# One fused fp32 kernel: two subtractions go from GpSimd to VectorE, and the hand-written order of all steps is written anew

## The chip, the cores and the metric

The kernel runs on one core of a Trainium2 chip. The metric is device microseconds for one execution; several executions are timed, and the median is compared. One more execution was recorded by the hardware profiler; all rows below come from it.

## The reference, cut to what matters

```python
def reference(x, state, moe_w_in, moe_w_out, moe_g_ln, moe2_w_in, moe2_w_out):
    y = attn(x, state)                  # 4 x 8 heads; two softmaxes, one over 32 states, one over 512 tokens
    y = y.transpose(0, 2, 1, 3).reshape(2176, 512)
    h = y @ moe_w_in                                   # 512 -> 1024
    solu = h * softmax(h)
    ln = layernorm(solu) * moe_g_ln
    z = ln @ moe_w_out                                 # 1024 -> 512
    h = z @ moe2_w_in                                  # 512 -> 2048
    g = h * tanh(softplus(h))
    return g @ moe2_w_out                              # 2048 -> 512
```

Everything is fp32.

## The kernel before, in words

An fp32 operand is split into a high part (a cast to fp32r) and a low part (operand minus high part), and a product is three matmuls: high by low, high by high, low by high. So nearly every operand that the PE takes costs a cast (mostly on ACT) and a subtraction (mostly on DVE) first. The host hands the weights over as 64-bit words, which `narrow` (L148 to L171) turns into fp32 in three or four steps on DVE and ACT; FLAGS B, T and W choose the engine and form of each.

The 2,176 tokens are 17 tiles of 128. For tile i, `a0(i)` is the matmul into `ph`, `a1(i)` the SoLU and LayerNorm (L557 maximum on DVE, L560 exponential on ACT, L562 product on DVE, L566 square on ACT, L568 to L572 small POOL steps, and the application to the 128x1024 tile: L580 on DVE where FLAGS N is 1, L575 on POOL and L577 on ACT where it is 0). `turn_far(i)` turns a tile through memory: L607 transposes 32x32 blocks on DVE into `tt`, L611 stores it (`td`), four L616 loads bring it back into `ln_l`, L618 casts to `ln_h` on ACT, L620 subtracts, 128x1024; FLAGS P chooses VectorE or GpSimd for that subtraction. `d(block, m)` multiplies with w_out (four quarters of six matmuls, L640) and copies the result out of PSUM (L645, `raw_a`, `raw_c`, `raw_d`; ACT or DVE by FLAGS X).

The second MoE layer runs in three passes over 6, 6 and 5 tiles, each with seven block products in place of eight. `x_split(pass, k)` makes the token operands (L811 difference, L816 cast on ACT, L818 subtraction on DVE). Pass 0 also prepares the 2 x 16 weight slices: `load64(0 or 1, f)` (L664, 512 KB from w2i or w2o, then narrow), `sums64` (L681), `split_in` and `split_out` (cast L705, L741 and subtraction L707, L743), `split_osum` (L748, L750, into `w2s`), and stores of the parts to device memory for passes 1 and 2, `keep_in` (L711) and `keep_out` (L754 for `w2s`, L757 for the rest). In a pass, for each of eight weight blocks: `hp` (L884, seven products of six matmuls into PSUM), `post` (L895 copies the first product to `m`, L898 and L901 add the next ones to `u`, L906 makes `c`), `act` (L918, L925 on ACT, L929), and `po` (L939 to L941 in pass 0, L989 to L996 later). The tile `m` of L895 may lie where `w2s` lay, so it must not be written before the stores of `w2s` have left it.

Nothing orders this work but two tables. FLAGS is a set of strings, a digit for each instance of an operation, read by `eng`, `on` and `copy_on`. ORDER is one string, two characters for an entry: each entry says which of the 1,040 step generators is advanced to its next `yield`. There are 3,182 entries. So each engine's queue, SP's DMA queue included, holds its instructions in the order of the table, and each engine takes its own queue strictly in order. A step is named here with its part: `turn_far(7).7` is the eighth part of that generator.

In the trace, 0 to 147 us are attention and the first layer (to tile 11), 147 to 222.7 us the last five tiles, the first x_split and the first weight slices, 222.7 to 340 us pass 0, 340 to 460 us pass 1 and 460 to 578 us pass 2.

Of the kernel before, what the change touches and what calls it, by code (L numbers as in the profile page):

```python
# [19 lines left out]
B, H, S, NS, D = 4, 8, 512, 32, 64  # L20
DM, FF1, FF2 = 512, 1024, 2048
NTOK = B * (S + NS)
P = 128
# [19 lines left out]
    A="1000",  # L43
    B="10101011000111100000000011100111",
    C="110000001000",
    D="00000",
# [20 lines left out]
    Y="00001111111111110",  # L67
    Z="11110111001100100",
# [10 lines left out]
    "CSBwCICWCZCSBwAsAsCJAuAuCSBwAwAwCWCSCJAyAyBuCZCZB0BuCWCWCWCLBuCLCJCaCdCWCLCWB0CaCJCLBwCGCGCTB0CWBwCdCdCaCICTBwCa"
    "BwCICaCaCTBxAlAlCeCXAnAnBxCaChApApCXArArBxCaCeB3CYCXB0ChChCaB3CeDMCYDMCHB3CeCICUCeCeCiDKDKCUCYCeCiB2CUCeB0B3CbCi"  # L80
    "CeDKDMCiB0CbB0CMB0CiCiDKCbDMB2B3CiCkB3CMCiB3CiB3CkCkB2DMCKClB5DKClDLCjCMB5DLClCjCgCKDLB5CgClClClCKCKDLCLCgAtAtCc"
    "B1ClAvAvDLCnAxAxCJCcClAzAzB1CcClCnCnB1B4B4CICqCoCMCICmCoCqCqCmCoCfDJCfDJCoCfCoCoCrDJDJCoB4CrCACjCoCjCoCrCjDPCjDP"
    "CmDJCpCACmCrDOCmCmCrCrDOCACpDOCrCrB9CjCrCtCjCsB9CtCtCsCmB9DPCuCwCmCuDPDOCuDPCMCwCwCMDOCuCuCuB6B6CxCuCuCzCuCxCNCz"
# [90 lines left out]
def attn_moe_kernel(ctx, tc, xT, xn, bd, stT, w_in, w_out, g_ln, w2i, w2o, out):  # L174
# [892 lines left out]
    def plan(step, *args):  # L1067
        steps.append((step, args))
# [71 lines left out]
    for ps in range(NPASS):  # L1140
# [93 lines left out]
```

## Time and profile before

| | us |
|---|---|
| runs | 575.02, 576.29, 577.04 |
| median | 576.29 |
| the profiled execution | 580.88 |
| its span, first to last instruction | 578.0 |
| PE, DVE, ACT, POOL busy in it | 557.9, 506.4, 355.6, 58.5 |

The profiled execution is 4.6 us above the median of the runs, and 2.9 us of it lie outside the span. Matmuls are pipelined and overlap in the records, so a busy PE isn't a PE at its peak; it is the stretches in which it isn't busy that can be read directly. A row of the time line is: start, duration, engine, line, operation, output and inputs, shape, count, and in brackets the idle time of the engine just before it with what ended it.

### The profile page before, as it was taken

The page shows a single profiled execution, that of the slowest core. Times are in us where ns is not written, and L with a number is a line of the kernel's source. Part 1 is how long each engine was busy: PE and PEld are TensorE (multiplying, and loading weights), DVE is VectorE, ACT ScalarE, POOL GpSimd, SP SyncE. Part 2 cuts the span into 40 slices and gives each one's busy share as a digit, 9 for nine tenths or more (in the row PEclk, how much of TensorE's full clock was granted, in tenths as well). Part 3 has the DMA queues.
Part 4 walks back from the last instruction along what each step waited for, and adds up shares of the span by engine and source line. Part 5 has one row for each costly group of instructions (what it writes and reads, how often), then busy time and mean ns, then how long its engine had stood idle before and what let it go on. Part 6 is the DMA issues. An engine that isn't in the chain of part 4 may idle for free.

```text
span 578.0 us, 9801 instructions
## 1 busy us (share of the span) xinstructions
PE 557.9 (97%) x3513; PEld 493.5 (85%) x3513; DVE 506.4 (88%) x956; ACT 355.6 (62%) x662; POOL 58.5 (10%) x132
## 2 busy tenths in 40 slices
PE   9899999999999796999999999999999999999997
PEld 4444877799689796888989989999999998999997
DVE  6999988984779686999999998679889999989996
ACT  6998966555467544999989774553334634533331
POOL 0003314121122000000000000000000015000023
PEclk9999999999999999999999999999999999999999
DMA  8962234053216777898999797967677679898842
GB/s 343 411 219 74 74 112 170 13 183 110 74 74 220 234 283 273 292 305 314 335 370 341 281 338 266 372 221 269 237 270 261 227 280 322 296 333 301 280 161 91
DMA packets 50015, 139.18 MB, mean 241 GB/s; under 512 B 5680, under 2 KB 22704, under 8 KB 49968
## 3 DMA queue, kind: packets, MB, share of 16 engines
q1 hardware_dynamic: 49968, 138.57, 67.7%
q8 instruction: 27, 0.44, 0.3%
q14 instruction: 20, 0.16, 0.1%
HBM read 98.18 MB, written 40.37 MB: 240 GB/s over the span
## 4 chain that ended last, share of the span: by engine, by line
PE 68%; DVE 13%; ACT 9%; DMA 6%; issue 2%; POOL 1%; SPq 0%; ACTq 0%; POOLq 0%; DVEq 0%
PE hp L884 27%; PE pm L640 8%; PE po L989 6%; PE po L990 6%; PE po L991 6%; PE po L940 3%; PE po L941 3%; PE po L939 3%; PE ph L548 3%; DMA w<-in_w2i 2%; ACT ph L566 2%; DVE ez L562 1%; DMA ko<-w2s 1%; PE po L1057 1%; DVE ez L580 1%
## 5 line engine op out<-in xcount | busy, mean ns | idle before, releaser
L884 PE MATMUL hp<-xo,w2r 128*128 128x384 f32 (+1 forms) x504 | 93.3, 329 | 0.3 <-DVE c L906 0.3
L884 PE MATMUL hp<-xo,w2swh 128*128 128x384 f32 (+1 forms) x336 | 83.8, 332 | 3.9 <-ACT m L895 3.9
L884 PEld LDWEIGHTS hp<-xo,w2r 128*128 128x128 f32 x504 | 84.3, 188 | 3.5 <-DVE c L906 1.1
L640 PE MATMUL pm<-ln_l,gw_hi 128*128 128x256 f32 (+1 forms) x256 | 76.3, 298 | 5.6 <-ACT raw_d L645 4.6
L640 PE MATMUL pm<-ln_h,gw_hi 128*128 128x256 f32 (+1 forms) x256 | 74.8, 292 | 0.0
L640 PE MATMUL pm<-ln_h,gw_lo 128*128 128x256 f32 (+1 forms) x256 | 74.5, 291 | 0.0
L996 DVE TENSOR_TENSOR acc<-po,acc 128x384 f32<-128x384 f32 (+1 forms) x136 | 68.7, 522 | 3.7 <-PE po L991 3.1
L884 PEld LDWEIGHTS hp<-xo,w2swh 128*128 128x128 f32 x336 | 60.7, 191 | 6.2 <-ACT m L895 4.2
L925 ACT ACTIVATE gh<-c 128x384 fp32r<-128x384 f32 (+1 forms) x57 | 29.2, 513 | 51.8 <-DVE c L906 44.1
L640 PEld LDWEIGHTS pm<-ln_l,gw_hi 128*128 128x128 f32 x256 | 48.2, 188 | 9.5 <-ACT raw_d L645 5.4
L884 PE MATMUL hp<-xo,w2swl 128*128 128x384 f32 (+1 forms) x168 | 55.8, 332 | 0.0
L963 ACT CAST qh<-t 128x384 fp32r<-128x384 f32 (+1 forms) x60 | 28.6, 489 | 37.5 <-PE po L991 21.4
L640 PEld LDWEIGHTS pm<-ln_h,gw_hi 128*128 128x128 f32 x256 | 48.2, 188 | 0.5
L906 DVE TENSOR_TENSOR c<-hp,u 128x384 f32<-128x384 f32 (+1 forms) x72 | 38.2, 532 | 11.9 <-PE hp L884 11.7
L640 PEld LDWEIGHTS pm<-ln_h,gw_lo 128*128 128x128 f32 x256 | 48.6, 190 | 0.0
L548 PE MATMUL ph<-swh,aT 128*128 128x512 f32 x128 | 45.1, 455 | 2.3 <-DVE swl L506 1.3
L989 PE MATMUL po<-ql,w2oh 128*128 128x384 f32 (+1 forms) x120 | 39.4, 328 | 0.2 <-DVE acc L996 0.2
L990 PE MATMUL po<-qh,w2oh 128*128 128x384 f32 (+1 forms) x120 | 38.8, 323 | 0.0
L991 PE MATMUL po<-qh,w2ol 128*128 128x384 f32 (+1 forms) x120 | 38.7, 323 | 0.0
L548 PEld LDWEIGHTS ph<-swh,aT 128*128 128x128 f32 x128 | 22.4, 188 | 14.2 <-issue 5.6
L965 DVE TENSOR_TENSOR ql<-t,qh 128x384 fp32r<-128x384 f32 (+1 forms) x59 | 31.1, 537 | 1.3 <-ACT qh L963 0.9
L884 PEld LDWEIGHTS hp<-xo,w2swl 128*128 128x128 f32 x168 | 32.0, 190 | 0.0
(458 smaller groups left out, 1349.1 us busy)
## 6 DMA issues: line engine op xcount, KB each, us to landing
w2r<-ki SPq DMA_DIRECT2D x16, 768.0 KB, 6.2
w2ol<-ko SPq DMA_DIRECT2D x15, 768.0 KB, 5.9
w2oh<-ko SPq DMA_DIRECT2D x15, 768.0 KB, 6.1
w<-in_w2i SPq DMA_DIRECT2D x16, 512.0 KB, 5.7
w2swh<-ki SPq DMA_DIRECT2D x8, 896.0 KB, 7.2
w2swl<-ki SPq DMA_DIRECT2D x8, 896.0 KB, 5.5
td<-tt SPq DMA_DIRECT2D x12, 512.0 KB, 2.7
ln_l<-td SPq DMA_DIRECT2D x48, 128.0 KB, 3.1
```

Source lines behind the costliest of these rows:

```text
L548: nc.tensor.matmul(out=ph[:, hf * 512:(hf + 1) * 512], lhsT=a_[:, c * P:(c + 1) * P], rhs=w_[:, q, hf * 512:(hf + 1) * 512], start=q == 0 ...
L640: nc.tensor.matmul(out=pm[:, :n], lhsT=w_[:, k, m * P:(m + 1) * P], rhs=l_[:, c0:c0 + 4 * len(blk), k, :], start=k == 0 and j == 0, stop=k ...
L884: nc.tensor.matmul(out=r, lhsT=w_[:, 0, k * P:(k + 1) * P], rhs=x_[:, k, :n], start=s in (0, 1, 3, 4) and cnt == 0, stop=cnt == 5, skip_gr ...
L906: nc.vector.tensor_tensor(out=c, in0=bank[ps, fp, s], in1=u, op=ALU.add)
L925: nc.scalar.activation(out=gh, in_=src, func=AF.Mish)
L939: nc.tensor.matmul(out=po["p", j], lhsT=gh[:, c], rhs=wl, start=first, stop=False)
L963: nc.scalar.copy(out=hi, in_=src)
L965: on('V', ((ps - 1) * NFP + fp) * 4 + int(name[1]) - 1).tensor_tensor(out=lo, in0=src, in1=f32(hi), op=ALU.subtract)
L989: nc.tensor.matmul(out=r, lhsT=wh[:, a, c], rhs=x[1], start=first or not held, stop=False)
L990: nc.tensor.matmul(out=r, lhsT=wh[:, a, c], rhs=x[0], start=False, stop=False)
L991: nc.tensor.matmul(out=r, lhsT=wl[:, a, c], rhs=x[0], start=False, stop=last or not held)
L996: on.tensor_tensor(out=o, in0=x, in1=y, op=ALU.add)
```

## The change

The same 1,040 steps are made, and ORDER has the same 3,182 entries in another order: no step is added or left out. One loop that lists the steps gets a condition on `STAGED`, which is empty, so the list stays the same. The digits of FLAGS that change move instances between engines: the two L620 subtractions that were on GpSimd (P, tiles 4 and 11) and one L965 subtraction (V) go to VectorE; of the L580/L577 applications tiles 3 and 11 go to VectorE and tiles 10, 14, 15 and 16 to ScalarE (N); five L564 (Z) go from GpSimd to VectorE; seven more L645 copies go from ScalarE to VectorE (X); the first two L895 copies go from ScalarE to VectorE (M); slice f=0 of w2i and the last w2o slice change the form of narrow (T).

```diff
 FLAGS = dict(
-    B="10101011000111100000000011100111",
+    B="00011111001011100001000001101110",
...
-    M="001000000010000001100000",
-    N="00000001101001111",
+    M="110000000001101000010000",
+    N="00010001100101000",
...
-    P="00001000000100000",
-    Q="101111011011110101010001",
+    P="00000000000000000",
+    Q="111011101111111101010001",
...
-    S="110011",
-    T="11001001100000001000111111111110",
+    S="101000",
+    T="11001001100000000000111111111111",
...
-    V="0000000000000000000000000001000000000000000000000000000000000000",
-    W="00100000000100100001101001000111",
-    X="01000000100000000001000000000100",
+    V="0000000000000000000000000000000000000000000000000000000000000000",
+    W="00000000011000000001100001001101",
+    X="00100000111100101001010000000101",
...
-    Z="11110111001100100",
+    Z="10000101000001001",
...
 ORDER = (
-    "AAAABIBIBKBKBQBQATBSBSBMBMARARAUAUBABABJBJBJBCBCBLBLBJBLBOBOBRBRAWAWATBLBWADADBRA-A-BTBTBXAJAJBTA0A0BNBRANANAYAY"
+    "AAAABKBKATBIBIBQBQBSBSBMBMBCBCBABAARARBLBLATAUAUBLAWAWBJBJBLBJBOBOBRBJBRANANBWBRA-A-BTBWADADBXBTA0A0BRAJAJBNBXBN"
...
         for fp in range(NFP):
-            if ps:
-                for d in range(2):
+            for d in range(2):
+                if ps or fp in STAGED:
                     plan(s_fetch_in, ps, fp, d)
+                if ps:
                     plan(s_fetch_out, ps, fp, d)
```

On DVE near 95 us, where the first of the two subtractions was made on POOL beside L580, the queue before was (L580 is the application to tile 7, L607 the block transpose, L506 the low part of the state weights, L557 the maximum of the next tile, L620 at the end that of another tile):

```order
L607 STREAM_TRANSPOSE tt<-ez 128x1024
L506 TENSOR_TENSOR swl<-ph,swh 128x2x512
L580 TENSOR_SCALAR ez<-ez,lnsm 128x1024
L607 STREAM_TRANSPOSE tt<-ez 128x1024
L506 TENSOR_TENSOR swl<-ph,swh 128x2x512
L557 TENSOR_REDUCE lnsm<-ph 128x1
L620 TENSOR_TENSOR ln_l<-ln_l,ln_h 128x1024
```

and now is

```order
L607 STREAM_TRANSPOSE tt<-ez 128x1024
L506 TENSOR_TENSOR swl<-ph,swh 128x2x512
L580 TENSOR_SCALAR ez<-ez,lnsm 128x1024
L607 STREAM_TRANSPOSE tt<-ez 128x1024
L620 TENSOR_TENSOR ln_l<-ln_l,ln_h 128x1024
L506 TENSOR_TENSOR swl<-ph,swh 128x2x512
L557 TENSOR_REDUCE lnsm<-ph 128x1
L620 TENSOR_TENSOR ln_l<-ln_l,ln_h 128x1024
```

One L620 more stands on DVE, between the transpose of tile 7 and the subtraction L506 for which the PE waits.

On DVE near 180 us, at the tiles 15 and 16 (the last L607 of each list is the transpose of tile 15, the L562 and L564 that of tile 16's statistics), the queue before was

```order
L557 TENSOR_REDUCE lnsm<-ph 128x1
L811 TENSOR_TENSOR raw_a<-raw_a 128x2x384
L580 TENSOR_SCALAR ez<-ez,lnsm 128x1024
L562 SCALAR_TENSOR_TENSOR ez,lnsm<-ph,ez 128x1024
L818 TENSOR_TENSOR xo_2016<-raw_a,xo_2016 128x768
L564 TENSOR_SCALAR lnsm<-lnsm 128x1
L607 STREAM_TRANSPOSE tt<-ez 128x1024
```

and now is

```order
L557 TENSOR_REDUCE lnsm<-ph 128x1
L811 TENSOR_TENSOR raw_a<-raw_a 128x2x384
L607 STREAM_TRANSPOSE tt<-ez 128x1024
L818 TENSOR_TENSOR xo_2004<-raw_a,xo_2004 128x768
L562 SCALAR_TENSOR_TENSOR ez,lnsm<-ph,ez 128x1024
L620 TENSOR_TENSOR ln_l<-ln_l,ln_h 128x1024
```

The application to tile 15 (L580) has left DVE for ACT, and the transpose of tile 15 stands ahead of the work on tile 16.

At the start of pass 0 the row of ACT before was (L816 the last x_split, L895 the first product to `m`, L705 casts of the next weights, L925 and L918 the first activation)

```order
L816 CAST xo_2520<-raw_a 128x768
L895 COPY m_2529<-hp 128x384
L705 CAST w2r<-w_2445 128x256
L925 ACT_TABLE_LOAD
L925 ACTIVATE gh<-hp 128x384
L918 ACTIVATE a__2554<-hp 128x384
```

and DVE's, in which L153 to L169 narrow the slice `load64(0, 3)`,

```order
L645 COPY raw_d<-pm 128x384
L153 TENSOR_SCALAR w_2445<-w_2445 128x512
L160 TENSOR_SCALAR w_2445<-w_2445 128x512
L165 SCALAR_TENSOR_TENSOR w_2445<-w_2445 128x512
L169 SCALAR_TENSOR_TENSOR w_2445<-w_2445 128x512
L818 TENSOR_TENSOR xo_2520<-raw_a,xo_2520 128x768
L898 TENSOR_TENSOR u_2542<-hp,m_2529 128x384
```

DVE's now is

```order
L645 COPY raw_d<-pm 128x384
L818 TENSOR_TENSOR xo_2499<-raw_a,xo_2499 128x768
L895 COPY m_2521<-hp 128x384
L707 TENSOR_TENSOR w2r<-w_2372,w2r 128x256
L707 TENSOR_TENSOR w2r_2502<-w_2372,w2r_2502 128x256
L153 TENSOR_SCALAR w_2452<-w_2452 128x512
L898 TENSOR_TENSOR u_2538<-hp,m_2521 128x384
```

The copy L895 has gone from ACT to DVE, right behind the last x_split, and the slice `load64(0, 3)` is narrowed behind it. By where the tiles lie, `m` there now overlaps another `w2s`, whose store left much earlier; the later one lies under the tile `u` that L901 writes.

## Rows read from the trace of the kernel before

**Rows 1.** By stretch: PE, weight loads, DVE, ACT, POOL busy; granted clock, DMA share, GB/s.

```profile
222.70:236.00 13.30, 9.41 (x45) 8.95 (x44) 8.98 (x20) 7.50 (x13) 0.00 (x0) 0.87 0.73 277
236.00:340.00 104.00, 103.59 (x514) 92.50 (x513) 102.08 (x221) 93.19 (x161) 0.00 (x0) 1.00 0.92 326
340.00:460.00 120.00, 120.00 (x673) 117.22 (x672) 103.78 (x203) 58.04 (x124) 1.02 (x1) 1.00 0.74 266
```

**Rows 2.** Time line near 95 us: POOL's subtraction, DVE beside it, PE.

```profile
95.19 2.41 POOL L620 TENSOR_TENSOR ln_l<-ln_l,ln_h 128x1024 fp32r<-128x1024 f32 x1
95.20 2.95 DVE L580 TENSOR_SCALAR ez<-ez,lnsm 128x1024 f32<-128x1024 f32 x1 [0.90 <-POOL lnsm L572]
100.59 0.72 PE L548 MATMUL ph<-swh,aT 128*128 128x512 f32 x2 [1.30 <-DVE swl L506]
106.64 0.81 DVE L580 TENSOR_SCALAR ez<-ez,lnsm 128x1024 f32<-128x1024 f32 x1 [0.20 <-POOL lnsm L572]
```

**Rows 3.** Time line 146 to 155 us: start of x_split, and POOL's second subtraction.

```profile
146.57 0.83 ACT L816 CAST xo<-raw_a 128x768 fp32r<-128x768 f32 x1 [1.93 <-PE tr L483]
147.43 0.96 DVE L818 TENSOR_TENSOR xo<-raw_a,xo 128x768 fp32r<-128x768 f32 x1 [6.36 <-ACT xo L816]
152.23 1.23 DVE L620 TENSOR_TENSOR ln_l<-ln_l,ln_h 128x1024 fp32r<-128x1024 f32 x1
153.37 4.02 DVE L818 TENSOR_TENSOR xo<-raw_a,xo 128x768 fp32r<-128x768 f32 x2
154.13 2.45 POOL L620 TENSOR_TENSOR ln_l<-ln_l,ln_h 128x1024 fp32r<-128x1024 f32 x1 [19.00 <-ACT ln_h L618]
```

**Rows 4.** Pieces of the chain that ended last, in order of time: start, us, what.

```profile
163.77 1.24 ACT ez L577
182.48 4.23 DMA td<-tt
186.73 6.72 DMA w<-in_w2i
220.97 7.20 DMA ko<-w2s
```

**Rows 5.** Time line 175 to 200 us: tiles 15 and 16, and who waits.

```profile
175.47 1.12 ACT L566 ACTIVATE ph<-ez,lnsm 128x1024 f32<-128x1024 f32 x1 [1.56 <-DVE lnsm L564]
181.22 1.23 DVE L607 STREAM_TRANSPOSE tt<-ez 128x1024 f32<-128x1024 f32 x1
193.53 0.67 ACT L155 ACTIVATE w<-w 128x512 f32<-128x512 f32 x1 [4.79 <-DMA w<-in_w2i]
196.82 0.39 PE L640 MATMUL pm<-ln_l,gw_hi 128*128 128x256 f32 x1 [2.69 <-ACT raw_d L645]
```

**Rows 6.** Time line 207 to 222 us: SP's issues, PE at block 7, DVE.

```profile
207.27 0.33 SPq L664 DMA_DIRECT2D w<-in_w2o  x1
207.70 0.38 SPq L711 DMA_DIRECT2D ki<-w2swh  x1
211.92 0.34 PE L640 MATMUL pm<-ln_l,gw_hi 128*128 128x384 f32 x1
211.97 0.43 DVE L153 TENSOR_SCALAR w<-w 128x512 f32<-128x512 f32 x1 [1.52 <-DMA w<-in_w2o]
221.14 0.55 DVE L645 COPY raw_d<-pm 128x384 f32<-128x384 f32 x1
```

**Rows 7.** Time line of the start of pass 0, and one stretch of it.

```profile
224.45 0.43 DVE L153 TENSOR_SCALAR w<-w 128x512 f32<-128x512 f32 x1 [2.76 <-DMA w<-in_w2i]
228.32 0.48 ACT L895 COPY m<-hp 128x384 f32<-128x384 f32 x1 [4.19 <-DMA ko<-w2s]
228.85 0.62 PE L884 MATMUL hp<-xo,w2swh 128*128 128x384 f32 x2 [3.89 <-ACT m L895]
230.00:232.00 2.00, 2.00 (x7) 2.00 (x7) 1.07 (x4) 1.83 (x4) 0.00 (x0) 0.50 0.97 348
233.65 0.51 PE L884 MATMUL hp<-xo,w2swh 128*128 128x384 f32 x2
```

More of the change, by code (lines that the diff above doesn't have):

```diff
@@ L79 @@
[L79 to L83, printed above, removed]
@@ new lines @@
+    "AgA3A5BjBjA5AiAiA9BdBhBhA5CDAdAdA5BnBnBFCDBdAfAfBiBiCCBrCEBFBdBkBHCCByBHBdCEBHBvBFBdCECCByBHBFBvCDByBlAhAhCEBeAj"
+    "AjBUBsBsBvBeBVCRBUBlAkAkCFBtAmAmBwBVBtCFAoAoCFCHCRCRAqAqBtCFCHBtCHCGCFCSBtCVCHCGBtCSBtCVCVBtBtCSCEBwCECWBzBzCSCS"
+    "CSCIBwCWCZCSBwAsAsCLAuAuCSBwAwAwCWCSCLAyAyBuCZCZCJBuCWB0CJCWCWBuCaCJCdCWCLCWB0CaCJBwCLCGCGB0CTBwCWCdCdCaCICTBwCa"
+    "BwCICaCaCTBxAlAlCeCXBxAnAnCaChApApCXBxCaArArCeCXChChB3CaCeCYB0CUCYB3DMCUCeCHB3DMCICeCeB0DKCiDKB3CeCeB2CYCiCUCMCe"
+    "DMCMCiB2DMCKDMCiCbB3CiCiDKB0B0DKB0CbCiCkB2DKCiCbCiCkCkB3B3B3DLClB5CjClDLCMCjClB5CgDLCKB5ClDLClClCKCKDLCnCgClAtAt"
@@ new lines @@
+    "B1AvAvCgB1ClAxAxCnCnClAzAzB1B4CqCoB4CLCcCmCoDJCICJCqCqCmCoCMCcCIDJCoCrCoCoCfDJB4CfCoCrDJCfCcCACoCmCoCrCmCmDPCmDJ"
+    "CpDPCjCrCACjDOCjCrCrCACjDOCpDOCrCrB9CmCrCtCsB9CmCtCtCsCjB9DPDOCuCwDOCjCuDPCuCwCwDPCuCuCuB6B6CxCMCzCuCuCxCNCMCzCz"
+    "B7CNCNCxCNDQCPDQB-DQCPC0CPDQCPB7DNC0CNCuDNDQC0DNDSB7DNB-B7DSCpDNB-CsDSC0B7CpC0C0DSCpCvCpDUB-CsC0CsB-DUCsC0B7C0Cv"
+    "DUB-B7B7C2CPCxB8CxCxB-B-DUB8DSCxC2C2CpB8CxCxDUDRCpDTCsCyDRDTC1CyDTCsC1CQDRCQC3DRDTDRC3CQCvDTCOCvC3DXCyCOCyDXCvC3"
+    "CvCOCOC3C3CyDXCyB_CQDXC3C3B_DYDXB_DYC3DVCvC4DYDVCyCvC4DVCyDYDVDYDWDVDWDWDWCQDpDpDqDqDqDbC1DtCQDWC1C5C1DvDtC1C4Dt"
@@ new lines @@
+    "DtDvC4DbC4DvDvC4C5DuDbDuDaC1DuDuC5C1C4C5C5C4DbC6C8DbC6C8C8C6DcC6C9DaC6C6DcC9C6DaC6C_C9C6C_C_C7C9C9C9DcC7DAC9C9Dc"
+    "C9DCDADcC-DCDCDAC-DaDADDDZDaDADADZDZDDDADZDADDDFDAC7C7C7DDDBDFDFC7DDDDC-C-DZC-DdDDDGDrC-DdDBDDDDDwDeDdDGDED0D1Dd"
+    "C7DrDrDeDEDxDeDdDGC-DeDwC7DfDGDGDGDfDeC-DfD0DGDfD0DgDfD1DgDGDGD0DgD0DgD1D8DhD1DBDgDxEBEBDwDwDhDBDjDED1DBDjD2D-DE"
+    "D2DBDjD2DED8D9DEDHD2D2ECECDhD9D_EFEFDjD-DyEDEDDxDhDjEGEGDxDiDhDxDBDkD_DiDEDBELEHEHDID3DkDED4DiDHDiDHDyDyDkDiD3Dy"
+    "DkDyDmDkDIDzD5DzDmDzDzDzD6DIDlD7D6ELEAEADlD4D7EMDlELELDlD5ELEIEEEEDmETDlEYEYETDmEcEcDnDmEMEMDnEMEIDnEMENEVDnENEZ"
@@ new lines @@
+    "EZENENENEUDoEWEUDnEaEaEVDoEJEIEdEdEWDoEIEfEeEeDoEIDoGpGpDsEOGrEPEXDsDsGrGsEjEPEiGrEOE5EJEJEbGsGtEJGrEJEfGtEKEfEQ"
+    "GrEKEfGsEKGrGtEREKEKGsGyGyESEREjGrGrEXEXGsEgGwESGvGxGxGwGsGsGzGzGvEQGuE2GvG9EbEbEjGuEiEjEfG9GwElEiG3G3GuEiG5G5Ej"
+    "G-G2G2EsEiE5G1G1EwEwEsEqG0G0ElE0E0EgG-G7G7EvEvEmEqFQE2G8G8EgEzEzEkG9EgEkEkEkEkG6G6ErE2EtEgG4G4G_ErExExG9G_FREhE2"
+    "E6EhG9EhG-EnG_EoG9G-FQEoHCG9G9G-HCEhEhHBHFHFEmEpE2E3HDHDHBEuEuE5G-G-HEHEE5FQHPEpFQHBHPE5HQFRFBHJHJHQFRFGFGEtHPE9"
+    "HCHAE1E1HAEnHPFQHRFNHREyEyHAHLHLFYHRHPFRHQFdFdFYHHHHE6FBFhFhE8HGHGFRFKFKE3FFE9HIHIFaE8E6HMHMFJE3E6FnHQHPFeFeFSFS"
@@ new lines @@
+    "E3HOHOE6HKHKE7FDE3FNHPHPFHFHFNHUE4FNE4HWHWE7E4HNHNHQE-E_HVHVHQHQFoHUE4E4HhE7HTE_HTHXHXFAE-FOE7E7FCFFFFHhFAHiFCFk"
+    "HSHhFJFJFnHTFDFEHcHcHiFnFLFLFEHdHdFIFIHSFnFNFMFMHhHSFTI7HbHbFUHiHjHZHZFoFTFSHYHYHjHUFZFOHhFSFSFOFZHhFOHiF-FnHhHh"
+    "FbHjFkHiFfFfHoHoFOHmHmHiHiHaHaHlFbHnHnHlFUFkFjFjHzFPHkFPFPFkI7HgHgI7HfHfFWHlFVHeHeFWHkFPFPH0HtHtFaFlFXHzFoFvF_Hm"
+    "FcFcFoHzF0F0H0FiFiFVFXHpHpH1FoH1F7HvHvFgFgF-F-HzFpFxFvF-F1F1HzH0F4F4H1FlHzH0HkH4HzHzI7H4I7H0HrHrFxH3HqHqH3FkF5F5"
+    "HsHsFpFrFpFqHuHuH0H0FwFzFrH6H6H2H3HyHyFqH2I7F3IFI7FlFpFpIAIAFlH2H5H5FwFyHwHwGVFlIGF2F2HxHxFyFsFmH-H-GWFmF6F6FmH7"
@@ new lines @@
+    "H7F-FtH_H_F_F_FsIBIBFmFmF_FtH9H9H4F8FuIFF7I7I7F7FzFzF_IFF7FuIGIEIEGSGGF3F3F7IDIDIHGLGLGAGIIFGAIHGMGMGIGCGVIFGQGQ"
+    "IGGVGAIHIFGBGVIGGAGAIFIFGBIKGGGHH8H8IGGPGPIKGHICICIJIGIGIJIMIMIKGJGWIXIIGNGNIJIIF8F8ILILGWIIF8ISISGVIRIRGCGWF8IN"
+    "INF9IPIPIYF9GdF9IVIVGWGiGiGEITITF9F9GSGXIQIQGSGEIWIWGFGXGTGdGfIXGXGSGmGmGJGjGjIXIYGRGRGDGXGXGeGKGKGFIOIOIZGSGgIX"
+    "GDIZGkGkGYGOGOIZIXGZGhGeIYIUIUGYIXIYGlGgIcIfIfIcGZGoGoIcIXIXIYGTIbIdIdGTJDJDIbIYIYJFJFIeIeGTIbIpGfIaGnGnGTIaIjIj"
+    "JiIaGaIlIlI8GUGUIqIiIiGUGUGUGbIkIkGcGbIgIgGhGhGcIpGaI8I8GlGlIpJAIqJAJAIpIrJAJAIrI8I8IoIoIqJBImImI9JBJBIpI9I9JBJB"
@@ L131 @@
+    "PIO5O4O7PJO6O7PIO6PNPNO8PJPIPIPNPMO8PMPDPDQAQAPJPJO9PMP-PLPlP-P-POPOPPPlPmPOPOPOPlPRO9PSPRO-PmO_O-PlPPPiPQPiPiPQ"
+    "PePePkO_PTPkPkPmPUPTPdPdPUPnPVPnPSPWPVPlPWPnPlPmPlPlPmPpPXPmPmPpPYPXPoQCPqPrPqPYPZQDPrPaPsPZQCPqPpPbPaQCPrQDPuPs"
+    "PgPgPbPcPuPfPfPtPcPwQBQBPtPxP_P_PwQCPxQEQEPrPrPyQEPvPzPvQCQDPyQCQDPyPzP0QDP1PzP0QGP6P1QGP2QHQGP7QHP2P3QHP4P4P3P8"
+    "P5P5P4QCQCP4QIP5QDQDP9QFP5QIQFQJP6QIP6P7QKQJQFQJP7QLP8QKQMP5QKP9QOQLQMP4QLQNQMQPQNQNQOQPQOQP"
 )
```

73 lines of the change are left out of this document (22 added, 51 removed).

## Prediction

> **What bounds the kernel now.** I read the stretches first, then the time line of each stretch in which the PE isn't busy, then the chain that ended last between them. The span is 578.0 us. From 236 us on the PE has no time to give: 103.59 us of 104 in pass 0, 120.0 of 120 in pass 1 [rows 1]. Pass 0 is tight on three sides: DVE is busy 102.08 of its 104 us and the DMA engines 0.92 of the time [rows 1]. So work saved inside the passes can't show, and a new wait there costs its full length. What can be won lies ahead of 236 us, in a few places where the PE stands still, and above all between 222.7 and 236 us, where it is busy 9.41 of 13.30 us and its granted clock means 0.87 [rows 1].
>
> Those places hang together. Between 147 and 229 us the chain runs from the last tiles' transposes through DMAs: the store of `td` takes 4.23 us, the weight slice that takes its room 6.72, and the store of `w2s` for which pass 0 waits 7.20 [rows 4]. ACT stood 4.19 us at L895 for that store (its tile `m` lies where `w2s` lay), and the PE 3.89 us behind it, for the second part of `hp` [rows 7]. After that gap the granted clock was 0.50 in the stretch 230 to 232 us, the lower level of 1.2 GHz [rows 7].
>
> **The change part by part.** The sum is a difference of waits, read in the profiled execution (span 578.0, 580.88 in all) and taken off the median of 576.29: the two differ by 4.6 us, which I take to be the same before and after.
>
> (a) *First subtraction back to DVE.* L620 took 2.41 us on POOL from 95.19, and the L580 that DVE began at 95.20 took 2.95 us, where the same shape took 0.81 at 106.64 [rows 2]. So DVE lost 2.14 us to a neighbour. On DVE the subtraction costs 1.23 [rows 3], and it stands ahead of the L506 for which the PE waited 1.30 [rows 2]: 2.14 − 1.23 = 0.9 us earlier, at most the 1.30 that the PE waited. Take 0.9.
>
> The Trainium skill, page "SBUF — State Buffer", section "Who interferes with whom", says that VectorE and GpSimd share one pair of ports, and that whoever begins first holds it for its whole instruction while the other is blocked. The trace agrees in the main: 2.14 us lost beside an instruction of 2.41. By the rule L580 would have lost all 2.41, and this term would be 1.2 in place of 0.9.
>
> (b) *Second subtraction.* At 154.13 it took 2.45 on POOL, while two L818 on DVE took 4.02 together; one alone took 0.96 [rows 3], so 2.1 was lost; on DVE it costs 1.23. Up to 0.9 earlier, but in the new order the tile's other steps stand between, so I count nothing, and keep 0.9 for the range.
>
> (c) *Start of x_split.* ACT waited 1.93 us for the PE's transposition L483 before the cast at 146.57, and DVE had idled 6.36 behind it [rows 3]. Now that transposition stands three quarters of a `d` block earlier in the PE's queue. That is longer than the wait ahead of the cast, so at most the 1.93 can go, and something else may be last then. Between 0 and 1.9, take half: 1.0.
>
> (d) *Tile 15 applied on ACT.* Its square ran at 175.47 for 1.12, to 176.6 [rows 5]. A cast of x_split (0.83) stands behind it on ACT, and the small POOL steps end about 1.2 us behind the square, as tile 12's did ahead of its L577 at 163.77; so the application, 1.24 [rows 4], runs from 177.8 to 179.0, and the transpose, now ahead of the next tile's work, follows at 179.0 in place of 181.22 [rows 5]: 2.2 us earlier. Store and slice load follow in chain [rows 4]. ACT waited 4.79 us at 193.53 for that slice, and the PE 2.69 at 196.82 for a copy that stood behind it on ACT [rows 5]; nothing stands in the way of passing the 2.2 on. Range 0 to 2.2.
>
> (e) *What is queued anew at 207 to 213 us.* In SP's queue the load of a w2o slice stood ahead of the store L711 (207.27, 207.70); now it stands behind it, and L711 waits for ACT's last `split_in`: some 0.8 us later. And `d(7, 1)`'s copy L645, on DVE before and now, has moved from the end of this stretch (221.14) to ahead of that slice's first step L153, which ran at 211.97 [rows 6]. The PE makes its last quarter now in the slot that began at 211.92 [rows 6] and ends about 213.0; then comes the copy. So DVE, whose queue holds the weights behind it, starts 1.6 us later, and up to 2.4 with the later load; the store of `w2s` follows. If the PE arrives early it costs nothing. Between 0 and −2.4, take −2.0, near the upper end, since the PE is held in the same chain as DVE.
>
> (f) *Start of pass 0.* L895 moves to DVE, right behind the last x_split, and its `m` lies over a `w2s` stored long before; now the L901 of the same block has to wait for the late store, and it is first needed by the sixth part of `hp`. Before, that part began at 233.65 [rows 7]: 5.5 us behind the landing (220.97 + 7.20 = 228.17). Now it can begin 0.1 + 0.6 (L901) + about 1.0 of DVE's queue behind the landing, at 1.7. That is 3.8 us, with the clock's fall in it, since parts three to five then run before the landing, with a gap of about 1 us in place of 3.89. L895 costs DVE 0.55 us twice where DVE idled 2.76 us shortly after (224.45) [rows 7].
>
> (g) *Everything else.* Seven L645 copies, two L895, five L564 and one L965 more on DVE, less the applications: counted operation by operation with the durations of their kind (0.55 for a copy [rows 6]), some 3 us of DVE work more and 2 of ACT's, spread over the span, and none more on DVE in pass 0. In pass 1 DVE has 16 us to spare in 120 [rows 1]. Counted at nothing, cover: that slack.
>
> Sum: 0.9 + 1.0 + 2.2 − 2.0 + 3.8 = 5.9 us; 576.3 − 5.9 = **570.4**.
>
> **The rivals.** *The start is won and pass 0 gives it back.* Pass 0 has its own clock: 326 GB/s at a DMA share of 0.92 [rows 1]. If what paces it is the remaining slice loads and the stores, DVE idles as the head start runs out. Against it: DVE itself has only 1.9 us idle there, so loads come in time. That gives back all but a remnant: 575 to 577.
>
> *Only the start of pass 0 counts*: (c) and (d) end in DMAs that share the engines and land no earlier, and (e) is not paid. 576.3 − 3.8 = 572.5, which lies in the forecast's range.
>
> *New waits in pass 0: slower.* ORDER is new throughout, and large reads are issued at other points. The price of a slice that comes late is the 2.76 us for which DVE stood at 224.45 [rows 7], and in pass 0 with DVE 98% busy each such wait goes to the end. Two of them (5.5) leave it just faster; from the third it is slower: 576.3 − 5.9 + 8.3 = 578.7. For it: the DMA at 0.92 has no room for a late start. Against it: DVE's work and its place among the loads is nearly the old one there.
>
> **How the numbers follow.** Forecast, with the case of (f) alone, 0.73; gain given back, 0.14; new waits, 0.13. What this kernel's runs can tell from no change is about 0.3%, 1.7 us: below 574.6 is faster, above 578.0 slower. Likely range: 0.9 to 1.3 from (a), 0 to 0.9 from (b), 0 to 1.9 from (c), 0 to 2.2 from (d), −2.4 to 0 from (e), 3.8 from (f): gains of 2.3 to 10.1, so 566.2 to 574.0. The range takes in the gain given back, to 577. Faster 0.73, same 0.14, slower 0.13.
>
> **What would show it.** In the profile after: (a) no L580 near 95 us above 0.9 us, and no PE wait of 1.3 at the next L548; (c) the L816 cast earlier than 146.57 by more than (a) brings; (d) the store of tile 15 near 178 us less (a) and (c), and ACT's 4.79 us wait shorter; (e) a DVE wait for the PE at L645 before 213 us; (f) no `hp` wait above 1.5 us and a granted clock of 1.00 in 222 to 236 us, with `hp`'s sixth part about 6 us earlier. Pass 0's length should stay at 104 us. The forecast is wrong if DVE shows DMA waits in pass 0 that sum to more than 3 us, or if the late store's landing moves later than 228.2.

## The result and the profile after

| | us |
|---|---|
| before, median | 576.66 (575.02 to 578.66) |
| changed, median | 570.32 (569.96 to 570.45) |
| ratio | 0.9887, 95% interval 0.9855 to 0.992 |
| profiled execution before, span | 580.88, 578.0 |
| profiled execution after, span | 570.37, 568.6 |

The change takes 6.3 us off the median; the prediction said 5.9 and 570.4. Between the two profiled executions the spans differ by 9.4 us. So the trace of before shows some 3 us more to win than its median, and that has to be explained too.

First, two stretches of the kernel before that [rows 1] doesn't have (length, then busy time of PE, weight loads, DVE, ACT and POOL, granted clock, DMA share, GB/s):

```profile
95.00:110.00 15.00, 13.06 (x88) 9.32 (x73) 13.50 (x16) 7.42 (x14) 3.69 (x6) 1.00 0.20 76
194.00:204.50 10.50, 6.78 (x55) 6.44 (x54) 9.14 (x15) 8.35 (x15) 0.00 (x0) 1.00 0.85 273
```

And the stretches of the changed kernel, to be held against these two and [rows 1]:

```profile
95.00:110.00 15.00, 15.00 (x107) 11.37 (x106) 13.03 (x17) 8.33 (x16) 2.33 (x8) 1.00 0.29 103
194.00:204.50 10.50, 10.50 (x72) 10.48 (x71) 10.29 (x20) 5.36 (x12) 0.00 (x0) 1.00 0.74 276
222.70:236.00 13.30, 12.43 (x62) 10.92 (x62) 12.69 (x29) 12.25 (x20) 0.00 (x0) 1.00 0.92 333
236.00:340.00 104.00, 103.25 (x515) 92.23 (x514) 101.51 (x219) 93.30 (x167) 0.00 (x0) 1.00 0.89 323
340.00:460.00 120.00, 120.00 (x683) 118.15 (x683) 103.62 (x204) 55.88 (x116) 0.00 (x0) 1.00 0.76 274
```

From 95 to 110 us and from 194 to 204.5 us the PE doesn't stand still any more (1.94 and 3.72 us before), and between 222.7 and 236 us its clock is granted in full (1.00 in place of 0.87). From 236 us on hardly anything has changed: DVE and PE are as full as before. The time from the start of the sixth part of `hp(0, 0)` to that of the last addition of the kernel is 341.0 us before (233.65 to 574.69) and 341.2 after (223.89 to 565.04). All of the gain lies ahead of that part, as the prediction had it.

The start of pass 0, against [rows 7]. The prediction calls the part of `hp` that waited 3.89 us there the second; twelve matmuls, two parts of six, stand ahead of it in the trace, so it is the third.

```profile
217.57 0.55 DVE L895 COPY m<-hp 128x384 f32<-128x384 f32 x1
218.17 0.62 PE L884 MATMUL hp<-xo,w2swh 128*128 128x384 f32 x2 [0.96 <-DVE m L895]
223.28 0.56 DVE L901 TENSOR_TENSOR u<-hp,u 128x384 f32<-128x384 f32 x1 [0.57 <-DMA ko<-w2s]
223.89 0.62 PE L884 MATMUL hp<-xo,w2swh 128*128 128x384 f32 x2 [0.87 <-DVE u L901]
```

The late store of `w2s` is now waited for by L901, and the sixth part of `hp` starts 0.7 us behind its landing (issued at 215.51 and landed 7.7 us later, at 223.2), where before it started 5.5 us behind it. The wait of 3.89 us is gone; waits of 0.96 and 0.87, and two smaller ones between, stand in its place.

And the chain ahead of it, against [rows 5] and [rows 6]:

```profile
176.07 1.25 DVE L607 STREAM_TRANSPOSE tt<-ez 128x1024 f32<-128x1024 f32 x1
178.61 0.33 SPq L664 DMA_DIRECT2D w<-in_w2o  x1
179.04 0.38 SPq L611 DMA_DIRECT2D td<-tt  x1
184.10 0.33 SPq L664 DMA_DIRECT2D w<-in_w2i  x1
188.70 0.69 ACT L155 ACTIVATE w<-w 128x512 f32<-128x512 f32 x1 [2.80 <-DMA w<-in_w2i]
206.63 0.56 DVE L645 COPY raw_d<-pm 128x384 f32<-128x384 f32 x1 [0.31 <-PE pm L640]
208.61 0.43 DVE L153 TENSOR_SCALAR w<-w 128x512 f32<-128x512 f32 x1 [1.42 <-DMA w<-in_w2o]
```

Tile 15's transpose is 5.2 us earlier (176.07 for 181.22), its store 3.4, the slice load's issue 2.6, and the slice itself is taken up 4.8 us earlier (188.70 for 193.53). Of the 5.2 us the store passes on only 3.4, because SP's queue now holds it up: the load of a w2o slice stands ahead of it, and that load waited 3.1 us for the store of tile 14 and left at 178.61, when the transpose of tile 15 was already done. Before, the store waited 1.5 us for the transpose. The PE's wait of 2.69 us at 196.82, for a copy behind the slice [rows 5], is gone.

### The profile page after: what moved, and what is told of

The parts are those of the page before. It is cut to its first block, busy times and chain, and to the rows that moved or that the text cites. A ratio compares the mean times of both kernels' runs of the same rounds, so it can differ in the third digit from the quotient of the medians.

```text
span 568.6 us, 9811 instructions
## 1 busy us (share of the span) xinstructions
PE 555.6 (98%) x3513; PEld 491.9 (87%) x3513; DVE 504.5 (89%) x964; ACT 358.4 (63%) x660; POOL 52.2 (9%) x128
## 5 line engine op out<-in xcount | busy, mean ns | idle before, releaser
L884 PEld LDWEIGHTS hp<-xo,w2swh 128*128 128x128 f32 x336 | 59.1, 188 | 6.4 <-DVE m L895 1.3
L925 ACT ACTIVATE gh<-c 128x384 fp32r<-128x384 f32 (+1 forms) x57 | 29.3, 516 | 51.8 <-DVE c L906 44.9
L965 DVE TENSOR_TENSOR ql<-t,qh 128x384 fp32r<-128x384 f32 (+1 forms) x60 | 32.0, 544 | 0.6 <-ACT qh L963 0.2
```

The lines of the kernel that those rows point to most:

```text
L884: nc.tensor.matmul(out=r, lhsT=w_[:, 0, k * P:(k + 1) * P], rhs=x_[:, k, :n], start=s in (0, 1, 3, 4) and cnt == 0, stop=cnt == 5, skip_gr ...
L925: nc.scalar.activation(out=gh, in_=src, func=AF.Mish)
L965: on('V', ((ps - 1) * NFP + fp) * 4 + int(name[1]) - 1).tensor_tensor(out=lo, in0=src, in1=f32(hi), op=ALU.subtract)
```

## The experiments

Kernels that were timed together share the runs of the kernel before, whose medians were 576.91, 577.39 and 579.03 in the three groups; its single runs spread from 574.7 to 581.1. The changed kernel and what is derived from it spread by 0.5 to 2.2 us. So small steps are told by undoing them in the changed kernel, whose times (570.32, and 570.22 in a control) are taken as the reference there. The three kernels that undo a step were timed in the second group, which has no run of the changed kernel, and one kernel that ran in two groups differed by 0.5 us between them (`y_start` and `y_start2` below); differences below 1 us are read with that in mind.

### Where the gain lies: the order spliced

Two kernels join the two orders at the last part of `hp(0, 0)`; the choices in FLAGS go with the order.

```diff
 x_new_then_old
 order up to the last part of hp(0,0):  changed kernel
-order behind it:                       changed kernel
+order behind it:                       kernel before
 x_old_then_new
-order up to the last part of hp(0,0):  changed kernel
+order up to the last part of hp(0,0):  kernel before
 order behind it:                       changed kernel
```

> The changed kernel's order and engine choices up to the sixth product of the first weight block of pass 0 (the last part of hp(0,0)), and behind it the order and choices of the kernel before. Theory (the gain lies ahead of pass 0 and in its first block, passes 0 to 2 only carry it): 569.5 to 571.5 us, the changed kernel's 570.3. Rival (the new order inside the passes brings the gain): 575 us or more.

> The reverse: the kernel before up to the last part of hp(0,0), the changed kernel's order and choices behind it. Theory: no gain, 575 to 578 us, with the PE's wait of about 3.9 us in the second part of hp still there. Rival: 570 to 572 us.

Measured: 571.93 us for the first (571.48 to 572.94; ratio to before 0.991, interval 0.9887 to 0.9933), 577.84 for the second (575.45 to 579.21; ratio 1.0001, interval 0.9977 to 1.0025). The old order ahead of pass 0 gives no gain with either order behind it; the new one gives 5.0 us in its group. The first missed its range by 0.4 us: from the sixth part of `hp` to the last addition the old order takes 342.6 us when it begins at 224.52, against 341.0 when it begins at 233.65. In the six traces with the old passes this length grows as the start gets earlier: 341.0 from 233.65 and 232.78, 341.5 from 229.46, 342.2 from 226.70, 342.4 from 224.44 and 342.6 from 224.52; with the new passes it is 341.0 to 341.3 in all that start between 222.9 and 230.7. So the old order gives up to 1.6 us of a head start back, and the new order of the passes is worth that much, and only that.

The second one's trace shows something else. Its first 200 us are those of the kernel before, and yet:

```profile
194.00:204.50 10.50, 10.43 (x75) 10.13 (x75) 8.62 (x16) 7.52 (x15) 0.00 (x0) 1.00 0.74 266
222.70:236.00 13.30, 10.97 (x46) 10.61 (x47) 8.65 (x20) 9.20 (x16) 0.00 (x0) 0.74 0.70 239
```

The PE is busy all through 194 to 204.5 us, where the first trace had waits of 2.69 [rows 5] and 1.03 us. The fall of the clock (0.74 here) is there as before, behind a wait of 3.57 us.

### The kernel before once more

```diff
 the kernel before, unchanged
```

> The kernel before once more, for a second look with a profile. In two runs that share its first 200 us the slice load load64(0, 0) landed some 3.4 us after its issue, and the PE's waits of 2.69 and 1.03 us near 197 us were gone; in the first profile it took 6.72. Theory (that late landing belongs to the first profiled execution, and not to the kernel): it lands within 4.5 us again, the PE is busy over 10 of the 10.5 us from 194 to 204.5, the wait at the second part of hp stays at 3 to 4 us. Rival (the load takes 6.7 us in the kernel before as a rule): PE busy under 8 of the 10.5 us.

Measured: 579.0 us in the one execution there is, and the theory fell: the slice was late again and the PE busy for 7.49 of the 10.5 us. But the time went elsewhere. The load itself took 4.6 us to land, just outside the theory's 4.5 and far from the rival's 6.7; it was the store ahead of it that took 5.6 in place of 4.23. The issues of store and load, the use of the slice, and the PE behind it, first in this trace and then in that of the kernel spliced from old and new:

```profile
182.94 0.33 SPq L611 DMA_DIRECT2D td<-tt  x1
188.59 0.33 SPq L664 DMA_DIRECT2D w<-in_w2i  x1
193.29 0.69 ACT L155 ACTIVATE w<-w 128x512 f32<-128x512 f32 x1 [3.67 <-DMA w<-in_w2i]
196.59 0.39 PE L640 MATMUL pm<-ln_l,gw_hi 128*128 128x256 f32 x1 [2.00 <-ACT raw_d L645]
```

```profile
182.44 0.33 SPq L611 DMA_DIRECT2D td<-tt  x1
186.08 0.33 SPq L664 DMA_DIRECT2D w<-in_w2i  x1
189.50 0.71 ACT L155 ACTIVATE w<-w 128x512 f32<-128x512 f32 x1 [0.78 <-DMA w<-in_w2i]
```

The same instructions in the same order: from the store's issue to the slice 10.35 us here, 11.05 in the first trace of before, 7.06 in the spliced kernel, 7.12 in the kernel `b_m` below. So the late slice doesn't belong to one execution, and it doesn't come with the order as a rule: both profiled executions of the kernel before have it (that of 580.88 us too), and the two kernels that share its first 200 us have the slice 3 to 4 us earlier. What decides it is open; `b_m` and the spliced kernel differ from the kernel before only behind that point. These 3 to 4 us are about half of the spread of the kernel before (6.4 us), but that they make this spread isn't shown: only executions with a profile show them.

### The two subtractions

In the kernel before, moved to DVE alone, and in the changed kernel, moved back to POOL alone:

```diff
 b_dve (the kernel before)
-    P="00001000000100000",
+    P="00000000000000000",
 u_pool (the changed kernel)
-    P="00000000000000000",
+    P="00001000000100000",
```

> The kernel before with its two L620 subtractions on DVE in place of POOL, at the places where the order names them: behind L580 near 95 us, and behind the two L818 near 154 us. Steps (a) and (b) by themselves. Prediction: L580 takes 0.81 in place of 2.95, the two L818 1.9 in place of 4.02, each L620 costs 1.23, so 0.9 us less at each place. The first place stands ahead of a wait of the PE, so 576.9 - 0.9 = 576.0, at most 575.1 with the second. Rival (the time is lost again in the store and slice load of 182 to 193 us): 576.5 to 577.5, with L506 near 99 us 0.9 earlier all the same.

> The changed kernel with its two L620 subtractions (tiles 4 and 11) on POOL again, all else as in the changed kernel. Theory of the prediction's (a) and (b): DVE loses some 2 us to its neighbour at each place and saves 1.2, so 0.9 us later at the first, up to 0.9 more at the second: 571.2 to 572.1. Rival (both places have room since the PE has d work to put there): 570.0 to 570.7.

Measured: `b_dve` 577.22 us against 579.03 (ratio 0.9971, interval 0.9949 to 0.9993: 0.4 to 3.0 us faster; the ranges had been written for 576.9, and the 0.9 to 1.8 us that they promise lie in it); `u_pool` 571.04 (570.42 to 571.25), 0.7 above the changed kernel and between the two ranges. The rows of `b_dve` at the two places, and the PE behind the first, against [rows 2] and [rows 3]:

```profile
95.97 0.81 DVE L580 TENSOR_SCALAR ez<-ez,lnsm 128x1024 f32<-128x1024 f32 x1 [0.90 <-POOL lnsm L572]
96.70 1.22 DVE L620 TENSOR_TENSOR ln_l<-ln_l,ln_h 128x1024 fp32r<-128x1024 f32 x1
98.99 1.18 DVE L506 TENSOR_TENSOR swl<-ph,swh 128x1024 fp32r<-128x1024 f32 x1
100.23 0.74 PE L548 MATMUL ph<-swh,aT 128*128 128x512 f32 x2 [0.17 <-DVE swl L506]
152.88 1.82 DVE L818 TENSOR_TENSOR xo<-raw_a,xo 128x768 fp32r<-128x768 f32 x2
155.75 1.22 DVE L557 TENSOR_REDUCE lnsm<-ph 128x1 f32<-128x1024 f32 x1
```

L580 takes 0.81 again, and L506 begins 3.02 us behind it in place of 4.15: 1.1 us won, and the PE's wait falls from 1.30 to 0.17. At the second place L557 begins 2.87 us behind the L818, 3.95 before: another 1.1.

In the changed kernel's order the same two instructions on POOL do no harm on DVE. POOL and DVE in `u_pool`:

```profile
99.39 2.39 POOL L620 TENSOR_TENSOR ln_l<-ln_l,ln_h 128x1024 fp32r<-128x1024 f32 x1 [3.23 <-ACT ln_h L618]
99.32 1.21 DVE L506 TENSOR_TENSOR swl<-ph,swh 128x1024 fp32r<-128x1024 f32 x1
100.45 1.21 DVE L557 TENSOR_REDUCE lnsm<-ph 128x1 f32<-128x1024 f32 x1
152.92 2.48 POOL L620 TENSOR_TENSOR ln_l<-ln_l,ln_h 128x1024 fp32r<-128x1024 f32 x1 [19.08 <-ACT ln_h L618]
153.95 1.22 DVE L557 TENSOR_REDUCE lnsm<-ph 128x1 f32<-128x1024 f32 x1 [0.80 <-PE ph L535]
```

There POOL's 2.4 us run beside L506 and L557, which read `ph` out of PSUM and take their usual 1.21 and 1.22. So the price lay in what stands beside the subtraction on DVE, and not in its being on POOL. The 0.7 us that `u_pool` loses don't come from these rows (L557 of tile 12 is even 0.26 earlier than in the changed kernel, 154.21). Nor do they come from the slice load, which is issued 1.3 us later (185.44 for 184.10) but used at the same time (188.78 for 188.70). The late store of `w2s` is issued 0.7 us later (216.19 for 215.51); what makes that is open, and two executions of the changed kernel itself differ by 0.7 us (570.37 and 569.71).

### The transposition ahead of x_split

```diff
 u_tr (the changed kernel), order of entries
+d(4,2).0 turn_far(10).2 d(3,1).4 turn_far(10).3 d(4,1).0 turn_far(10).4 d(4,2).1 turn_far(10).5 turn_far(11).2
 back(3,1).4
...
-d(4,2).0 turn_far(10).2 d(3,1).4 turn_far(10).3 d(4,1).0 turn_far(10).4 d(4,2).1 turn_far(10).5 turn_far(11).2
```

In the changed kernel the nine entries of the last line don't stand together; they are spread over some thirty entries behind `back(3,1).4`.

> The changed kernel with the three quarters of block d(4) and their neighbours put ahead of the transposition L483 of back(3, 1) again, as they stood before: step (c). Theory: x_split begins up to 1.9 us later, and so do tiles 12 to 15 and the PE behind them: 570.3 + 1.0 to 2.0 = 571.3 to 572.3. Rival (DVE and ACT make it up before 200 us): 570.0 to 570.7.

Measured: 572.21 us (571.33 to 573.55), 1.9 above the changed kernel and in the theory's range. The first cast of x_split, in the changed kernel and in this one:

```profile
143.55 0.83 ACT L816 CAST xo<-raw_a 128x768 fp32r<-128x768 f32 x1 [2.65 <-PE tr L483]
```

```profile
145.46 0.83 ACT L816 CAST xo<-raw_a 128x768 fp32r<-128x768 f32 x1 [1.92 <-PE tr L483]
```

1.9 us later at the cast, 1.9 at tile 12's L557 (156.12 for 154.21), 1.3 at the first `hp`, and 1.9 in the time.

### Tile 15 applied on ACT

```diff
 u_15 (the changed kernel)
-    N="00010001100101000",
+    N="00010001100101010",
 order of entries
-turn_far(15).0 load64(1,0).0 load64(1,1).0
...
-turn_far(15).1 load64(0,0).0
...
 a1(16).3
+turn_far(15).0 load64(1,0).0 load64(1,1).0 turn_far(15).1 load64(0,0).0
```

> The changed kernel with tile 15 applied on DVE again and its transpose, with the store and the slice load that follow, behind tile 16's statistics: step (d). The prediction's price: 2.2 us in the chain of store and slice load, 572.5. Rival, from the traces since: the store and the load take as much longer as they start earlier, so the slice is narrowed within 0.8 us of the old time and nothing is lost: 570.0 to 571.0.

Measured: 571.14 us (570.45 to 571.71), 0.8 above the changed kernel, far from the prediction's 572.5 and 0.1 outside the rival's range; the two kernels' runs overlap. SP and ACT in it:

```profile
181.32 0.33 SPq L611 DMA_DIRECT2D td<-tt  x1
183.94 0.33 SPq L664 DMA_DIRECT2D w<-in_w2i  x1
187.08 0.70 ACT L155 ACTIVATE w<-w 128x512 f32<-128x512 f32 x1 [0.20 <-DMA w<-in_w2i]
```

The store is issued 2.3 us later than in the changed kernel, and the slice is there 1.6 us earlier (187.08 for 188.70): store and load take 5.8 us from issue to use in place of 9.7. The 0.8 us don't lie there. In the trace 0.3 us are there long before, at 144.87 for 144.60 in the first product of the last tile, where the two kernels are still the same; and the PE has one wait that the trace of the changed kernel hasn't:

```profile
183.32 0.38 PE L640 MATMUL pm<-ln_l,gw_hi 128*128 128x256 f32 x1 [0.46 <-ACT raw_d L645]
```

So of step (d) the runs leave some 0.5 us, which is no more than they can tell.

### The first tile of pass 0, off the late store

In the kernel before, three other tiles take their room first, so that `m` comes to lie elsewhere; L895 stays on ACT.

```diff
 b_m (the kernel before), s_post
+        early = {name: temp(ps, name) for name in (("u3", "c2", "c1") if (ps, fp) == (0, 0) else ())}
         m1_ = temp(ps, "m1")
...
-        u3 = temp(ps, "u3")
+        u3 = early["u3"] if "u3" in early else temp(ps, "u3")
...
-            c = temp(ps, name)
+            c = early[name] if name in early else temp(ps, name)
```

> The kernel before with one thing changed: the first tile m of pass 0 is given its room after the tiles u and c of later products, so that L895 no longer has to wait for the store of w2s that leaves last; L895 stays on ACT, order and engines stay. Step (f) of the prediction by itself. Theory: the PE's 3.9 us wait at hp and the fall of the clock go, hp's sixth part comes about 3.8 us earlier behind the landing, 576.3 - 3.8 = 572.5 us. Rival (another wait, for the slice load of 224 us or for DVE's x_split of 226.6 us, is as late): 575 us or more.

Measured: 574.75 us (572.87 to 576.59; ratio 0.9962, interval 0.9935 to 0.9989: 0.6 to 3.8 us faster), between the two ranges. The PE's one wait left at `hp`, the sixth part of `hp`, and the stretch (lines behind L894 are one higher in this kernel):

```profile
224.24 0.62 PE L884 MATMUL hp<-xo,w2swh 128*128 128x384 f32 x2 [1.56 <-DVE u L899]
226.70 0.52 PE L884 MATMUL hp<-xo,w2swh 128*128 128x384 f32 x2
222.70:236.00 13.30, 11.48 (x53) 9.18 (x54) 13.17 (x30) 12.55 (x19) 0.00 (x0) 1.00 0.93 339
```

The wait is 1.56 in place of 3.57 in the execution with the same first 200 us, the clock stays at 1.00, and the sixth part begins 9.0 us behind the issue of the late store; in the traces with the old place of `m` that is 12.0 to 13.3 us, in the changed kernel 8.4. So the mechanism is shown and worth 3 to 4 us at this point. Of that 2.2 us reach the median; the old passes give part back, as in the splice (342.2 us from the sixth part to the last addition, where it was 341.0).

### Three steps alone

```diff
 b_three (the kernel before)
+the edits of b_dve and b_m
 order of entries
-d(4,2).0 turn_far(10).2 d(3,1).4 turn_far(10).3 d(4,1).0 turn_far(10).4 d(4,2).1 turn_far(10).5 turn_far(11).2
 back(3,1).4
+d(4,2).0 turn_far(10).2 d(3,1).4 turn_far(10).3 d(4,1).0 turn_far(10).4 d(4,2).1 turn_far(10).5 turn_far(11).2
```

> The kernel before with three edits: the two subtractions on DVE (a, b), the transposition L483 of back(3, 1) three quarters of d earlier (c), and the first tile m off the late store (f). Nothing else of the new order. If the three steps make the gain and add up: 576.9 - 0.9 - 1.9 - 2.2 = 571.9. Rival (each only moves the wait to the next place of the same chain): 574 us or more, no better than m alone, 574.75.

Measured: 571.23 us (570.37 to 571.99; ratio 0.9856, interval 0.9832 to 0.988): 7.8 us below the kernel before in its group, 579.03, where the changed kernel is 8.8 below. With nothing else of the new order the kernel comes within 1.0 us of the changed one (570.22 in the same group). Its wait for `u` at the start of pass 0 and the stretch:

```profile
222.00 0.61 PE L884 MATMUL hp<-xo,w2swh 128*128 128x384 f32 x2 [1.09 <-DVE u L899]
222.70:236.00 13.30, 13.00 (x62) 10.43 (x61) 13.17 (x30) 12.76 (x21) 0.00 (x0) 1.00 1.00 353
```

The three edits make nearly all of the gain, 7.8 of 8.8 us. By themselves, in three groups, they were worth 1.8, 1.9 and 2.2, which is 5.9; so together they bring at least what they bring apart, and whether the 1.9 us more are real isn't shown, since the kernel before itself differs by 2.1 us between these groups. What is left for all the rest of the new order, (d) and (e) with it, is 1.0 us.

### The first 39 us

The trace after shows the first token matmul 1.5 us later than that of before; the prediction had counted the new order of the first loads at nothing. Before, after, and in the control `c_after`:

```profile
38.37 1.98 PE L548 MATMUL ph<-swh,aT 128*128 128x512 f32 x4
```

```profile
39.84 1.98 PE L548 MATMUL ph<-swh,aT 128*128 128x512 f32 x4
```

```profile
38.74 1.98 PE L548 MATMUL ph<-swh,aT 128*128 128x512 f32 x4
```

```diff
 y_start and y_start2 (the same kernel)
-order up to a0(0), with its FLAGS:  changed kernel
+order up to a0(0), with its FLAGS:  kernel before
```

> The kernel before's order up to the first token matmul a0(0), at about 39 us, and the changed kernel behind it. The profile of the changed kernel shows that a0(0) 1.5 us later than before, which the prediction counted at nothing. Theory (that delay is carried to the end, since the PE is dense behind it): 570.3 - 1.5 = 568.8 us. Rival (the delay of the first 40 us is scatter of one execution, or is absorbed by the DMA chain of 176 to 215 us): 570.0 to 570.6 us.

> The changed kernel again, as a control beside the next one on the same chip: 570.0 to 570.8.

> The changed kernel with the old order of the first 39 us, beside the changed kernel on the same chip. If the later start is worth what the first comparison gave (569.25 against 570.32): 0.8 to 1.4 us faster than the control. Rival (the two differ by scatter between sessions): within 0.4 us of it.

Measured: `y_start` 569.25 us (568.6 to 570.84); beside each other, the control 570.22 (569.71 to 570.83) and `y_start2` 569.78 (569.37 to 570.25). The 569.25 lies between the two ranges; the 0.4 us of the pair are what the rival allows. The control's first token matmul is at 38.74, that of `y_start2` at 38.98, so in this pair the 1.5 us are gone, and 0.4 us are left with ranges that overlap. But the delay wasn't that of one execution. Four more kernels here have the new start, and they begin at 39.53 to 40.30; only the control is early. The eight traces with the old start begin at 38.37 to 39.15. So the new start is later in five of six traces, by 0.9 us in the mean. What that is worth in the time is open: the kernel with the old start came out lower both times, by 1.1 and 0.4 us, the first of them not beside its control.

## Why the prediction was right, point by point

The time was right because the place was right: the waits ahead of the sixth part of `hp` go, and the rest carries the head start. The sum of 5.9 came so close to 6.3 by luck: its errors cancel.

- (a), (b): taken as 0.9 and 0; in the old order they are 1.1 and 1.1 in the trace, 0.4 to 3.0 us in the time. By the rule of the Trainium skill (page "SBUF — State Buffer", section "Who interferes with whom"), which the prediction set beside (a), it would have been 1.2; the measured 1.1 lies between. Leaving (b) out was wrong: the step that failed is "the tile's other steps stand between". In the new order the harm wouldn't have arisen (0.7 us by `u_pool`, for a cause that isn't shown). The sign that it named is there: L580 takes 0.81 in the changed kernel (at 96.18), and the PE doesn't wait from 95 to 110 us.
- (c): taken as 1.0, half of the bound of 1.9. It is the whole 1.9, at the cast, at tile 12 and in the time. Nothing else was last.
- (a) to (c) in the trace: tile 12's L557 is 3.1 us earlier (4.2 in the control, which starts 1.1 us earlier than that trace); 1.1 + 1.1 + 1.9 = 4.1. Taken as 1.9.
- (d): 2.0 us earlier at the transpose, nearly as worked out (5.2 for all of (a) to (d), 6.2 in the control). But "nothing stands in the way of passing the 2.2 on" is the step that failed. SP's queue stood in the way: the store left 3.0 us behind the start of the transpose, where it had been 1.3, held by a load that waited for tile 14's store; so 3.4 of 5.2 us were passed on. And the DMAs behind it scatter by more than the step: store and load take 5.8 to 11 us from issue to use in these traces, in no order that the traces show. Undoing (d) costs 0.8 in the median, 0.3 of it at a place ahead of the edit, and the slice lands earlier without it. Both traces of the changed kernel have the slice in use at 188.3 to 188.7, the four that share the first 200 us of before at 189.5 to 193.5.
- (e): taken as −2.0; it is about nothing. From the slice's first use to the issue of the late store it is 27.4 us in the first trace of before and 26.8 after (26.5 to 28.0 in all traces with the old order there, 26.7 to 27.4 with the new one, and 29.6 in `u_15`, which has its slice earliest). DVE waited 0.31 us for the PE at the copy, since the PE came to it 6.5 us earlier, and 1.42 for the load, where it had waited 1.52 [rows 6]. The prediction saw "if the PE arrives early it costs nothing" and took the other end.
- (f): taken as 3.8 behind the landing, with the sixth part 1.7 us behind it; it is 4.8 in the trace (5.5 less 0.7), with the clock's fall gone in all traces with the new place of `m`. In the time, alone and with the old passes, it is 2.2.
- (g): pass 0 to the end took 341.0 and 341.2 us. Right for the new order. The rival "pass 0 gives it back" is true of the old order, up to 1.6 us.
- Not in the sum: the later start, 1.5 us in the profiled execution and 0.9 in the mean of the traces.

In the trace the sixth part is 9.8 us earlier: 4.8 by (f), and 5.0 since the late store lands at 223.2 in place of 228.2. Against the execution of the spliced kernel with the early slice, where that part began at 230.71, it is 6.8, close to the median's 6.3. So the step at fault in the sum's frame is the one that the prediction took for granted, that the profiled execution stands to its median by the same 4.6 us before and after: it had the slice 3 to 4 us later than two other executions of the same first 200 us, and the changed kernel's stands 0.05 above its median. That the late slice made the difference isn't shown: the second profiled execution of the kernel before had it too, and stood 1.6 us above its group's median of 577.39. Had (a) to (f) been sized right in that trace, taking the sum off the median would have promised 566.5.

## What to carry to other kernels

Price a step by what stands beside it and behind it: the same instruction on POOL cost 2.1 us of DVE beside one set of neighbours and nothing beside another. A transfer made ready earlier leaves earlier only if its queue lets it: here 1.7 of 5.2 us were lost behind another load. Ask of a first write into a tile what lay there before; a tile laid elsewhere left a wait of 1.6 us where one of 3.2 to 3.9 had been, and no fall of the clock, without moving any instruction. And before taking a wait in a profiled execution off a median, look whether a second execution has it: here ACT's 4.79 us for the slice and the PE's 2.69 behind it were there in two executions of the kernel before (3.67 and 2.00 in the second) and not in two others of the same first 200 us.

## What the runs showed of the hardware

L620 on POOL took 2.39 to 2.48 us in every trace that has it there, twice its 1.22 on DVE, and beside it L580 (128x1024, SBUF to SBUF) took 2.95 in place of 0.81 and two L818 (both inputs in SBUF) 4.02 in place of 1.82, while L506 (one input in PSUM and one in SBUF) took 1.21 and L557 (reading PSUM alone) 1.21.

The Trainium skill, page "SBUF — State Buffer", section "Who interferes with whom", says that a VectorE instruction with at most one SBUF input, outside the modes that use both ports, doesn't contend with GpSimd, and one with two does where GpSimd reads SBUF. The trace agrees on both kinds, by L506 and L557 in the rows of `u_pool` and by the two L818 of [rows 3]. L580 [rows 2] has one such input and was slowed all the same; in which mode it ran no run here shows.

The granted clock fell to a mean of 0.74 to 0.87 between 222.7 and 236 us in each of the four traces in which the PE had waited 3.2 to 3.9 us at the third part of `hp`, with 0.50, the lower level, in the stretch of [rows 7]; where the longest wait there was 1.56 us or less, it stayed at 1.00.

A store of 512 KB and the load of 512 KB behind it took from 5.8 to 11.1 us from the first issue to the use of the data; in the four traces with the same first 200 us alone it was 7.06, 7.12, 10.35 and 11.05.

SP's queue kept its order: the store of tile 15, whose transpose began at 176.07 and took 1.25, left at 179.04, right behind the load of 178.61 that had waited 3.1 us.
